# A fused attention and feed-forward kernel: strip one's first product taken set by set, three sets at two levels

## The chip, the cores and the metric

The kernel runs on one core of one Trainium2 chip. The metric is the device time of one execution in microseconds (us); the time of a kernel is the median of its runs. The engines are called as in the profile: PE (TensorE, the matmuls), PEld (its weight loads), DVE (VectorE), ACT (ScalarE), POOL (GpSimd) and SP (SyncE, which issues nearly all DMA transfers here).

## The reference

Everything is float32. An attention without softmax is followed by a feed-forward layer with a squared relu:

```python
# q, k, v: (8, 8, 576, 64); w_in: (512, 2048); w_out: (2048, 512)
kv = np.einsum('bhsd,bhse->bhde', k, v)
out = np.einsum('bhsd,bhde->bhse', q, kv)
rms = np.sqrt(np.mean(out * out, axis=-1, keepdims=True) + 1e-06)
out = out / rms * g_norm
x = out.transpose(0, 2, 1, 3).reshape(4608, 512)
h = np.maximum(x @ w_in, 0.0)
return (h * h) @ w_out
```

## The kernel before

**Strips.** The 4608 rows of x are 36 tiles of 128 rows, taken as nine strips of four tiles. Each strip has a first product (x with w_in, "up"), relu and square, and a second product (with w_out, "down"). While PE works on one strip, the attention that makes the next strips' x is slipped between its matmuls as *slices*: `transposed_query` (DVE turns a query tile), `key_value` (PE makes the 64 by 64 key-value products, ACT copies them), `query` (PE multiplies queries with them), then the mean, the inverse root and the scaling (DVE, or ACT for `scaled_heads`), and last either `features` (PE transposes the tile, ACT copies it into xT) or `squares_x` and `send_x` (DVE turns it in blocks of 32, the tile is stored to DRAM and later fetched back into xT by `fetch_x`). The list `slices` fixes their order; `attend(n)` issues them up to the n-th.

**Seven products for eight.** Every large product is computed by a Strassen-like scheme: x and w_in are cut in halves both ways, and seven products of sums and differences stand for eight. `A_IN` says in which of the seven blocks `b` of the tile `w_in` the operand of product `p` lies: 1:0, 2:2, 3:6, 4:3, 5:4, 6:5, 7:1. All blocks of all sets stay in the tile w_in. The quarters of the result are called 11, 12, 21 and 22 (tiles gt).

- *One level* (strip one before, `up`): for each of four column groups g, the seven products p in the order 1, 2, 6, 5, 7, 3, 4. Each has four matmuls with 128 by 128 weights and 256 columns of x. Three PSUM banks A, B, C collect them; ACT copies what is needed twice (snap), DVE adds two banks and applies relu and square in a second operation within SBUF.
- *Two levels* (strips two to eight, `up_slot` and `up_small`): the products are taken set by set, in the order `UP_SETS` = 1, 6, 7, 5, 2, 3, 4. Each set p is itself cut into seven small products j, of four matmuls with 128 columns. They are spread over 55 slots; set n takes the slots 7n, 7n+2, ..., 7n+12. A small product adds to what other sets left in the quarters (`UP_TO`), so no set has to be kept. The small products need sums of x (`sum_x`, `leaf_x`, on POOL) and, for j in 5, 6, 3, further sums of the weights.
- *Further sums of the weights* (`deep_sums_in(b)`, L1181): three POOL operations per block b make them from w_in, and one store (three for b = 0) writes them to the DRAM tensor w_in_deep, from which strips two to eight load them for each set. `deep_differences_in(b)` (L1200) overwrites one quarter of the block in w_in by a difference; it must come after every one-level use of the block and before its two-level use. Before the change the further sums are made during strip one (L1418, one block every third product, in the order b = 1, 6, 5, 4, 0, 2, 3) and the differences during strip two (L1253).

The second product of strips one to eight is `down_deep`: seven sets in the order 4, 1, 2, 6, 5, 7, 3, each of seven small products whose weights are read from DRAM (`w_blk`, two blocks per set of 0.79 and 1.05 MB, issued by `stream`). In strips two to eight the first three small products of its first set are issued within the last slots of up; in strip one before the change they are not.

**What sets the order.** There is no run-time scheduler: each engine works off its instructions in the order in which the loop at the end of the kernel (L1333 on) issues them, and waits on semaphores for operands and for buffers. SP issues the transfers in that order too, and each waits for the one eight places before it to land, so at most eight are under way. The pools matter: `stream_pool` has six buffers of 1 MB, shared by the w_blk blocks, the further sums while they are made, and the xT of each strip; `sum_pool` has eight buffers of 256 KB, for sums of x, of g (the operands of the second product) and parts of w_deep; `fpsum` has five PSUM banks from strip one on; the bank `x` that `query` writes is a single one. q, k and v loads are spread by a clock of the program's own (`clock`, `drip`, `keys_due`, `tiles_due`), which counts work issued, not time.

In strip one, before the change, the 28 steps of up and 14 of down are accompanied by this:

```python
if s == DEEP:
    attend(begun + (goal - begun) * min(i + 1, 25) // 25)
...
if s == 1 and i in range(2, 23, 3):
    deep_sums_in((1, 6, 5, 4, 0, 2, 3)[i // 3])
if s == 1 and i in (17, 20, 21, 23):
    stream()
```

Of the kernel before, what the change touches and what calls it, by code (L numbers as in the profile page):

```python
# [10 lines left out]
FP32 = mybir.dt.float32  # L11
# [9 lines left out]
def kernel(  # L21
# [34 lines left out]
    nc = tc.nc  # L56
# [593 lines left out]
    def send_x(n):  # L650
        d = sent[n] = dram.tile([P, 4, NP, SQ], FP32, name="x_d", tag="x_d", bufs=2 * NT)
        nc.sync.dma_start(out=d, in_=squared.pop(n))
        tiles_due.append((clock[0] + {9: 30, 10: 36, 11: 24}.get(n, 6), fetch_x, (n,)))

# [51 lines left out]
    slices += [(query_means, (last,)), (K, (2, 0, 1)), (T, (2, 0)), (roots_normalized, (last,)), (T, (2, 1))]  # L706
    slices += [(T, (2, 2)), (T, (2, 3)), (features, (last[0],)), (K, (2, 2, 3))]
    pair_ends = []
    for b in range(2, B):
        pairs = query_pairs(b)  # L710
        for i, pair in enumerate(pairs):
            left = len(pairs) - i
            more = b + 1 < B
            at = left + (b == 2)
            keys = (b + 1, *{2: (0, 1), 1: (2, 3)}[at]) if more and at < 3 else ()
            if i == 0 and b > 2:
                slices += [(T, (b, p)) for p in (2, 3)]
# [170 lines left out]

    def up(s, g, p):
        open_bank(p)  # L890
        rhs = {
            1: halves(s, 0, 0), 2: halves(s, 1, 0), 3: halves(s, 1, 1),
            4: xc[s][3], 5: xc[s][0], 6: xc[s][1], 7: xc[s][2],
        }[p]
        for i in range(2):
            product(p, i, lambda kc: w_in[:, kc, g, A_IN[p], ts(i, P)], lambda kc: rhs[:, :, kc, :], KH)
        dest = quarters(s, g)

        def relu_squared(q):
            def f(b, a):  # L900
                o = dest[q]
                nc.vector.tensor_tensor(out=o, in0=b, in1=a, op=ALU.add)
                nc.vector.scalar_tensor_tensor(out=o, in0=o, scalar=0.0, in1=o, op0=ALU.max, op1=ALU.mult)
            return f

        def last(b):
            nc.scalar.activation(dest[21], b, AF.Relu)
            nc.scalar.activation(dest[21], dest[21], AF.Square)

        combine(p, relu_squared(11), relu_squared(12), last, relu_squared(22))  # L910

# [190 lines left out]
    def down_deep(s, k, i):  # L1102
        p = DEEP_ORDER[k]
        if k == i == 0:
            stream()
        if s == N_STRIP - 1 and k == 6 and i == 1:
# [19 lines left out]
            return  # L1126
        if k == 0 and s >= DEEP_UP:
            if i == 0:
# [50 lines left out]
    w_half = lambda b, kc, f: w_in[:, kc, 2 * f : 2 * f + 2, b]  # L1179

    def deep_sums_in(b):  # L1181
# [7 lines left out]
        nc.gpsimd.tensor_tensor(out=s1, in0=w_half(b, 0, 1), in1=w_half(b, 1, 1), op=ALU.add)  # L1189
        minus(nc.gpsimd, s2, s1, w_half(b, 0, 0))  # L1190
        minus(nc.gpsimd, s4, w_half(b, 1, 0), s2)
        if b == 0:
            for n, x in enumerate((s1, s2, s4)):
                nc.sync.dma_start(out=w_in_deep[b, :, n], in_=x)
# [46 lines left out]
    def up_slot(s, slot):  # L1241

        for n, p in enumerate(UP_SETS):
            i, odd = divmod(slot - 7 * n, 2)
            if not odd and 0 <= i < 7:
                up_small(s, n, p, ORDER[i], slot)
# [86 lines left out]
    for s in range(N_STRIP):  # L1333
# [25 lines left out]
        for i, (w, fn, a) in enumerate(steps):  # L1359
# [33 lines left out]
            if s:  # L1393
                clock[0] += 3.2 if i >= n_up else 2.2 if s == DEEP else 1.2
                soon = tiles_due and tiles_due[0][2][0] // NT == s + 1
                if i == n_up + 10:
                    while tiles_due and tiles_due[0][2][0] // NT == s + 1:
                        _, f, a = tiles_due.popleft()
                        f(*a)
                elif not due(keys_due) and not (soon and due(tiles_due)):  # L1400
                    least = 2.1 if s == DEEP else 4.5 if i < n_up else 3.3
                    quiet = n_up * 2 // 3 < i < n_up + 3 or s == DEEP and i > n_up + 9
                    quiet = quiet or s == DEEP and i < n_up and drips and drips[0][0] == load_q_rest
# [15 lines left out]
                if s == 1 and i in (17, 20, 21, 23):  # L1419
                    stream()  # L1420
# [59 lines left out]
```

## Time and profile before

| what | value |
|---|---|
| median of 3 runs | 886.89 us (886.82 to 887.32) |
| profiled execution, its own time | 886.17 us |
| its span, first to last instruction | 884.4 us |
| granted clock of PE | 1.000 |
| strip one: up | 138.6 to 195.9 us |
| strip one: down | 195.9 to 236.9 us |
| strip two begins | 236.9 us |
| HBM read / written | 197.66 / 36.70 MB |
| mean transfer rate over the span | 265 GB/s |

The span runs from the first to the last instruction on the engines; the profiled execution's own time has 1.8 us more around it. Times in the views are counted from the start of the span. The chain of waits is followed back from the last instruction; where it runs through PE, PE had no time to spare. In it, and in counts of PE's instructions, every float32 matmul shows as two pieces.

### The profile page before, as it was taken

To read this page: it belongs to the slowest core of one execution; us is meant where nothing else is said; L and a number is where in the kernel's file an instruction comes from. 1 tells how busy PE (TensorE), PEld (TensorE's weight loads), DVE (VectorE), ACT (ScalarE), POOL (GpSimd) and SP (SyncE) were. 2 spreads that over 40 slices of the span, in tenths; PEclk is the share of its full clock that TensorE was granted. 3 is DMA by queue.
4 is the path that set the end of the run, shared out by engine and by line. 5 is a ranking of instruction groups with operands and counts; after the bars stand their busy time and mean duration, and the time that the engine had idled before them with its cause. 6 is when DMAs were issued, how large, how long until landed. Compare 5 with 4: busy or idle time off the path is not lost.

```text
span 884.4 us, 20899 instructions
## 1 busy us (share of the span) xinstructions
PE 876.4 (99%) x8296; PEld 822.1 (93%) x8296; DVE 721.9 (82%) x1239; ACT 351.8 (40%) x805; POOL 307.6 (35%) x316
## 2 busy tenths in 40 slices
PE   8999999999999999999999999999999999999998
PEld 7445888889999999999999999999999999999998
DVE  4999998879778985798778966897888778866887
ACT  4898242320048203740365034902491147102710
POOL 0000005610549133631474045604570447044700
PEclk9999999999999999999999999999999999999999
DMA  9998997999969996989677978897668765884482
GB/s 306 321 314 252 299 376 222 289 346 353 301 186 278 327 330 214 227 323 314 208 216 293 314 237 244 286 319 244 207 218 303 255 212 184 294 292 164 178 314 105
DMA packets 170257, 235.73 MB, mean 267 GB/s; under 512 B 79536, under 2 KB 134576, under 8 KB 161840
## 3 DMA queue, kind: packets, MB, share of 16 engines
q1 hardware_dynamic: 169856, 234.33, 81.0%
q8 instruction: 65, 1.06, 0.5%
q14 instruction: 32, 0.26, 0.1%
q10 hardware_dynamic: 304, 0.07, 0.0%
HBM read 197.66 MB, written 36.70 MB: 265 GB/s over the span
## 4 chain that ended last, share of the span: by engine, by line
PE 95%; DVE 2%; ACT 2%; issue 0%; POOL 0%; DVEq 0%; POOLq 0%
PE ps_B L1066 22%; PE ps_A L1283 19%; PE ps_A L1066 17%; PE ps_B L1283 9%; PE ps_A L839 6%; PE ps_C L1283 5%; PE ps_B L839 3%; PE kv_ps L432 2%; PE ps_A L880 2%; PE x_ps L468 2%; PE ps_C L839 2%; PE ps_C L880 2%; PE ps_B L880 1%; PE ps_A L617 1%; ACT gt L1234 0%
## 5 line engine op out<-in xcount | busy, mean ns | idle before, releaser
L1066 PE MATMUL ps_B<-w_blk,g_s 128*128 128x128 f32 x1008 | 123.9, 275 | 0.0
L1066 PEld LDWEIGHTS ps_B<-w_blk,g_s 128*128 128x128 f32 x1008 | 118.1, 192 | 0.1
L1283 PE MATMUL ps_A<-x_l,w_in 128*128 128x128 f32 x784 | 103.8, 275 | 0.3 <-ACT snap L1300 0.3
L289 POOL TENSOR_TENSOR x_l<-xT 128x256 f32<-128x256 f32 x21 | 15.7, 747 | 236.7 <-PE ps_A L1066 187.8
L1283 PEld LDWEIGHTS ps_A<-x_l,w_in 128*128 128x128 f32 x784 | 95.4, 192 | 0.6 <-ACT snap L1300 0.5
L1066 PE MATMUL ps_B<-w_blk,gt 128*128 128x128 f32 x752 | 95.2, 275 | 0.0
L1066 PE MATMUL ps_A<-w_blk,g_s 128*128 128x128 f32 x768 | 93.6, 275 | 0.0
L1066 PEld LDWEIGHTS ps_B<-w_blk,gt 128*128 128x128 f32 x752 | 89.6, 192 | 0.1
L1066 PEld LDWEIGHTS ps_A<-w_blk,g_s 128*128 128x128 f32 x768 | 89.6, 192 | 0.0
L1295 POOL TENSOR_TENSOR snap<-snap,gt 128x512 f32<-128x512 f32 x35 | 45.8, 1309 | 118.8 <-ACT snap L1300 103.7
L1300 ACT COPY snap<-ps_A 128x512 f32<-128x512 f32 x63 | 36.9, 585 | 109.7 <-PE ps_A L1283 98.0
L1233 ACT ACTIVATE gt<-gt 128x512 f32<-128x512 f32 x112 | 70.1, 625 | 12.8 <-DVE gt L1295 12.7
L1066 PE MATMUL ps_A<-w_blk,gt 128*128 128x128 f32 x576 | 72.2, 275 | 0.0
L1234 ACT ACTIVATE gt<-gt 128x512 f32<-128x512 f32 x112 | 70.7, 631 | 3.6
L1066 PEld LDWEIGHTS ps_A<-w_blk,gt 128*128 128x128 f32 x576 | 68.2, 192 | 0.0
L1082 ACT COPY o_sb<-ps_A 128x128 f32<-128x128 f32 x24 | 6.4, 265 | 148.4 <-PE ps_A L1066 148.4
L1081 DVE TENSOR_TENSOR o_sb<-o_sb,ps_B 128x256 f32<-128x256 f32 (+1 forms) x123 | 47.5, 386 | 16.9 <-ACT o_sb L1082 12.0
L289 DVE TENSOR_TENSOR gt<-gt 128x2048 f32<-128x2048 f32 (+1 forms) x29 | 59.7, 2064 | 0.0
L1295 POOL TENSOR_TENSOR gt<-gt,snap 128x512 f32<-128x512 f32 x42 | 52.3, 1273 | 17.8 <-DVE snap L1295 17.8
L1283 PE MATMUL ps_B<-x_l,w_blk 128*128 128x128 f32 x392 | 52.1, 276 | 0.0
L1283 PE MATMUL ps_A<-x_l,w_blk 128*128 128x128 f32 x392 | 51.9, 275 | 0.0
L1081 DVE TENSOR_TENSOR o_sb<-o_sb,ps_A 128x256 f32<-128x256 f32 (+1 forms) x96 | 37.2, 387 | 15.1 <-ACT o_sb L1082 10.5
(193 smaller groups left out, 1822.3 us busy)
## 6 DMA issues: line engine op xcount, KB each, us to landing
w_blk<-w_deep SPq DMA_DIRECT2D x56, 1024.0 KB, 6.6
w_blk<-w_out SPq DMA_DIRECT2D x56, 768.0 KB, 6.0
w_blk<-w_in_deep SPq DMA_DIRECT2D x49, 768.0 KB, 5.3
raw<-in_moe_w_in_dram SPq DMA_DIRECT2D x16, 512.0 KB, 7.1
raw<-in_moe_w_out_dram SPq DMA_DIRECT2D x16, 512.0 KB, 6.1
k<-in_k_dram SPq DMA_DIRECT2D x29, 256.0 KB, 4.6
v<-in_v_dram SPq DMA_DIRECT2D x29, 256.0 KB, 5.0
x_d<-x_q SPq DMA_DIRECT2D x27, 256.0 KB, 4.6
```

The source lines that it names most:

```text
L289: eng.tensor_tensor(out=out, in0=a, in1=b, op=ALU.subtract)
L432: nc.tensor.matmul(ps[ts(h, D), i], lhsT=a, rhs=w, start=i == 0 and c == 0, stop=c == C, skip_group_check=True)
L468: nc.tensor.matmul(ps[half, r, i, ts(p, D)], lhsT=q[row, half], rhs=kvd[b, p][row, row], start=True, stop=True)
L839: nc.tensor.matmul(bank[BANK[p]][:, i, :], lhsT=lhsT(k), rhs=rhs(k), start=p in (1, 5, 2) and i == 0 and k == 0, stop=k == n - 1, skip_gro ...
L880: nc.tensor.matmul(ps, lhsT=w_in[:, kc % KH, g, kc // KH * 2 + fh, ts(i, P)], rhs=xt[0][:, :, kc, :], start=kc == 0, stop=kc == NP - 1,)
L1066: nc.tensor.matmul(chain[c][x][:, i, :], lhsT=a[:, f, :], rhs=w[:, f, :], start=x not in opened[c] and f == 0, stop=f == FQ // 2 - 1, skip ...
L1081: add = lambda out, a, b: nc.vector.tensor_tensor(out=out, in0=a, in1=b, op=ALU.add)
L1233: nc.scalar.activation(o, o, AF.Relu)
L1234: nc.scalar.activation(o, o, AF.Square)
L1283: nc.tensor.matmul(ps[:, i, :], lhsT=w, rhs=rhs, start=j in (1, 2, 5) and i == 0, stop=True, skip_group_check=True)
L1295: add = lambda eng, out, a, b: eng.tensor_tensor(out=out, in0=a, in1=b, op=ALU.add)
L1300: nc.scalar.copy(t, ps)
```

## The change

Strip one's first product goes set by set. The sets 1, 6, 7 and 5 stay at one level: the new function `up_set(s, g, p)` runs the four matmuls of one group into one bank (ps_D), and adds from PSUM to the quarters (set 1 by an ACT copy; set 5 ends with relu and square of quarter 22 on ACT). The sets 2, 3 and 4 are done at two levels by `up_slot` in the slots 28 to 54, as in the later strips; the last three products of set 5 alternate with the first four slots. The first three small products of the second product's first set move into the slots 49, 51 and 53, so the weights for it are streamed earlier.

For this, the further sums of all blocks are made in another order and place (b = 6, 2, 3, 1, 5, 4, 0 at the steps 1, 3, 5, 7, 10, 13, 15), those of blocks 6, 2 and 3 stay in their stream buffers as weights of strip one, and the stores go out from a queue of their own some steps later. The differences of blocks 2, 6 and 3 move from strip two to strip one. A leaf of x is made for each of the three sets.

Around it, the attention of strip one changes: the first ten slices go one per product, the rest over the remaining 13 units of work; tile 8 goes through DRAM (`squares_x`, `send_x`, fetched when 50 units of the clock have passed) instead of `features`; the two pairs of batch two are scaled on ACT (`scaled_heads`) instead of DVE.

```diff
-        tiles_due.append((clock[0] + {9: 30, 10: 36, 11: 24}.get(n, 6), fetch_x, (n,)))
+        tiles_due.append((clock[0] + {8: 50, 9: 30, 10: 36, 11: 24}.get(n, 6), fetch_x, (n,)))
...
-    slices += [(T, (2, 2)), (T, (2, 3)), (features, (last[0],)), (K, (2, 2, 3))]
+    slices += [(T, (2, 2)), (squares_x, last), (T, (2, 3)), (K, (2, 2, 3)), (send_x, last)]
...
-                slices += [(T, (3, 1))] * (left == 1) + [(mean_roots, (pair,)), (normalized, (pair,))]
-                slices += [(T, (3, 0))] * (left == 2) + [(squares_x, (n,)) for n in pair]
+                slices += [(T, (3, 1))] * (left == 1) + [(mean_roots, (pair,)), (inverse, (pair,))]
+                slices += [(scaled_heads, (pair, t, r)) for t in range(2) for r in range(2)]
+                slices += [(T, (3, 0))] * (left == 2)
                 for n in pair:
-                    slices.append((send_x, (n,)))
+                    slices += [(squares_x, (n,)), (send_x, (n,))]
...
-    def up(s, g, p):
...
+    def up_set(s, g, p):
+        rhs = {1: lambda: halves(s, 0, 0), 5: lambda: xc[s][0], 6: lambda: xc[s][1], 7: lambda: xc[s][2]}[p]()
+        ps = fpsum.tile([P, 2, TH], FP32, name="ps_D", tag="f")
         for i in range(2):
+            for kc in range(KH):
+                nc.tensor.matmul(
+                    ps[:, i, :], lhsT=w_in[:, kc, g, A_IN[p], ts(i, P)], rhs=rhs[:, :, kc, :],
+                    start=i == kc == 0, stop=kc == KH - 1, skip_group_check=True,
+                )
         dest = quarters(s, g)
+        add = lambda q, a: nc.vector.tensor_tensor(out=dest[q], in0=ps, in1=dest[a], op=ALU.add)
+        if p == 1:
+            nc.scalar.copy(dest[11], ps)
+        elif p == 5:
+            add(22, 21)
+            add(12, 12)
+            nc.scalar.activation(dest[22], dest[22], AF.Relu)
+            nc.scalar.activation(dest[22], dest[22], AF.Square)
+        else:
+            add(*{6: (12, 11), 7: (21, 12)}[p])
...
-        if k == i == 0:
+        if k == i == 0 and s >= DEEP_UP:
             stream()
...
-        if k == 0 and s >= DEEP_UP:
+        if k == 0:
...
-            if k == 0:
-                nc.vector.tensor_tensor(out=q12, in0=q12, in1=q22, op=ALU.add)
...
+            if UP_SETS[4:].count(IN_SET[b]):
+                w_blk["in", DEEP, IN_SET[b]] = whole.rearrange("p n f e -> p n (f e)")
...
-        nc.sync.dma_start(
-            out=w_in_deep[b].rearrange("p n g e -> p n (g e)"), in_=whole[:, 0:3].rearrange("p n f e -> p n (f e)")
+        sums_to_store.append(
+            (w_in_deep[b].rearrange("p n g e -> p n (g e)"), whole[:, 0:3].rearrange("p n f e -> p n (f e)"))
         )
...
-        if s == DEEP_UP and at == 0 and n < 7:
+        if at == 0 and n < 7 and (s == DEEP_UP and n < 4 or s == DEEP and n > 4):
             deep_differences_in(A_IN[UP_SETS[n]])
...
-            steps = [(1, up, (s, g, p)) for g in range(NG) for p in ORDER]
+            x_sums[s, 4] = xc[s][3]
+            by_set = [(2, up_set, (s, g, p)) for p in UP_SETS[:4] for g in range(NG)]
+            small_ones = [(1, up_slot, (s, slot)) for slot in range(28, 55)]
+            steps = by_set[:13] + small_ones[:1] + by_set[13:14] + small_ones[1:3] + by_set[14:15]
+            steps += small_ones[3:5] + by_set[15:] + small_ones[5:]
...
-                    attend(begun + (goal - begun) * min(i + 1, 25) // 25)
+                    gone = min(int(passed[min(i, n_up - 1)]), 23)
+                    attend(begun + min(gone, 10) + max(gone - 10, 0) * (goal - begun - 10) // 13)
...
-                if s == DEEP and i == n_up - 3:
-                    leaf_sums(s, 4)
-                if s == 1 and i in range(2, 23, 3):
-                    deep_sums_in((1, 6, 5, 4, 0, 2, 3)[i // 3])
-                if s == 1 and i in (17, 20, 21, 23):
+                if s == DEEP and i in (1, 3, 5, 7, 10, 13, 15):
+                    deep_sums_in({1: 6, 3: 2, 5: 3, 7: 1, 10: 5, 13: 4, 15: 0}[i])
+                if s == DEEP and i in (3, 5, 7, 9, 11, 14, 26):
+                    for _ in range(3 if i == 26 else 1):
+                        out_ap, in_ap = sums_to_store.popleft()
+                        nc.sync.dma_start(out=out_ap, in_=in_ap)
+                if s == DEEP and i == 8:
+                    leaf_x(s, 4)
+                if s == DEEP and i == 9:
+                    deep_differences_in(2)
+                if s == DEEP and i in (18, 22):
                     stream()
```

More of the change, by code (lines that the diff above doesn't have):

```diff
@@ L887, in up_first @@
             nc.scalar.activation(dest[(11, 12, 21, 22)[2 * fh + th]][:, i, :], ps[:, ts(th, TH)], AF.Square)
-    def up(s, g, p):
[L890 to L894, printed above, removed]
-        for i in range(2):
-            product(p, i, lambda kc: w_in[:, kc, g, A_IN[p], ts(i, P)], lambda kc: rhs[:, :, kc, :], KH)
-        dest = quarters(s, g)
[L899 to L910, printed above, removed]
+    def up_set(s, g, p):
+        rhs = {1: lambda: halves(s, 0, 0), 5: lambda: xc[s][0], 6: lambda: xc[s][1], 7: lambda: xc[s][2]}[p]()
+        ps = fpsum.tile([P, 2, TH], FP32, name="ps_D", tag="f")
+        for i in range(2):
+            for kc in range(KH):
[3 more added lines that the diff above has]
+                )
+        dest = quarters(s, g)
+        add = lambda q, a: nc.vector.tensor_tensor(out=dest[q], in0=ps, in1=dest[a], op=ALU.add)
[8 more added lines that the diff above has]
+            add(*{6: (12, 11), 7: (21, 12)}[p])
     for p, t in zip((1, 2, 5), w_first):
@@ L1179 @@
     w_half = lambda b, kc, f: w_in[:, kc, 2 * f : 2 * f + 2, b]
+    IN_SET = {b: p for p, b in A_IN.items()}
+    sums_to_store = deque()
     def deep_sums_in(b):
@@ L1193, in deep_sums_in @@
             for n, x in enumerate((s1, s2, s4)):
-                nc.sync.dma_start(out=w_in_deep[b, :, n], in_=x)
+                sums_to_store.append((w_in_deep[b, :, n], x))
             return
-        nc.sync.dma_start(
-            out=w_in_deep[b].rearrange("p n g e -> p n (g e)"), in_=whole[:, 0:3].rearrange("p n f e -> p n (f e)")
+        sums_to_store.append(
+            (w_in_deep[b].rearrange("p n g e -> p n (g e)"), whole[:, 0:3].rearrange("p n f e -> p n (f e)"))
         )
@@ L1244, in up_slot @@
             i, odd = divmod(slot - 7 * n, 2)
-            if not odd and 0 <= i < 7:
+            if not odd and 0 <= i < 7 and (s > DEEP or n >= 4):
                 up_small(s, n, p, ORDER[i], slot)
@@ L1345 @@
         else:
-            steps = [(1, up, (s, g, p)) for g in range(NG) for p in ORDER]
+            x_sums[s, 4] = xc[s][3]
[3 more added lines that the diff above has]
+            steps += small_ones[3:5] + by_set[15:] + small_ones[5:]
+            small_steps = {28, 30, 32, 34, *range(35, 55)}
+            work = [2 if fn == up_set else a[1] in small_steps for _, fn, a in steps]
+            passed = [sum(work[: i + 1]) / 2 for i in range(len(steps))]
         n_up = len(steps)
@@ L1393 @@
             if s:
-                clock[0] += 3.2 if i >= n_up else 2.2 if s == DEEP else 1.2
+                clock[0] += 3.2 if i >= n_up else 1.1 * work[i] if s == DEEP else 1.2
                 soon = tiles_due and tiles_due[0][2][0] // NT == s + 1
@@ L1399 @@
                         f(*a)
-                elif not due(keys_due) and not (soon and due(tiles_due)):
+                elif not (due(keys_due) and (s > DEEP or due(keys_due) or True)) and not (soon and due(tiles_due)):
                     least = 2.1 if s == DEEP else 4.5 if i < n_up else 3.3
-                    quiet = n_up * 2 // 3 < i < n_up + 3 or s == DEEP and i > n_up + 9
+                    quiet = s > DEEP and n_up * 2 // 3 < i < n_up + 3
+                    quiet = quiet or s == DEEP and (i > n_up + 9 or i < n_up + 3 and passed[min(i, n_up - 1)] > 19)
                     quiet = quiet or s == DEEP and i < n_up and drips and drips[0][0] == load_q_rest
```

## The prediction

> **What bounds the kernel now.** I read the page's shares first: TensorE (PE) works 876.4 of 884.4 us, and the chain of waits is 95% PE. So a change pays where it takes work from PE, and costs where PE starts to wait. Then I took the stretch that is changed, strip one's first product, from the table of windows and the chain.
>
> ```profile
> PE 876.4 (99%) x8296; PEld 822.1 (93%) x8296; DVE 721.9 (82%) x1239; ACT 351.8 (40%) x805; POOL 307.6 (35%) x316
> ```
>
> ```profile
> 138.60:195.90 57.30, 57.27 (x511) 49.33 (x511) 45.90 (x71) 16.50 (x34) 29.62 (x21) 1.00 0.94 283
> 152.00:176.00 24.00, 23.96 (x204) 20.59 (x203) 20.27 (x32) 7.64 (x15) 15.78 (x12) 1.00 1.01 292
> 183.00:196.00 13.00, 13.00 (x63) 11.48 (x62) 10.39 (x20) 3.20 (x7) 0.00 (x0) 1.00 1.00 355
> ```
>
> The columns are the stretch, its length, then busy time (and count) of PE, PEld, DVE, ACT, POOL, the clock, the DMA share and GB/s. PE never stops in these 57.3 us, and neither do the DMA engines: share 0.94 to 1.01. PE and DMA are both full here; only ACT and POOL look free. The prices of PE's pieces come from the chain (start, duration, line, pieces; one float32 matmul counts as two pieces):
>
> ```profile
> 149.91 1.73 PE ps_B L839 x8
> 156.82 0.44 PE xt_ps L636 x4
> 158.98 1.46 PE kv_ps L432 x40
> 195.86 6.25 PE ps_B L1066 x56
> ```
>
> Four matmuls of 256 columns take 1.73 us. Seven products of four matmuls of 128 columns take 6.25, so one takes 0.893. What the other engines pay comes from their timelines, POOL's first, then a line each of ACT's and PE's:
>
> ```profile
> 142.77 1.27 POOL L1189 TENSOR_TENSOR w_i<-w_in 128x512 f32<-128x512 f32 x1 [58.81 <-DVE w_in L289]
> ...
> 147.04 1.71 POOL L1189 TENSOR_TENSOR w_i<-w_in 128x512 f32<-128x512 f32 x1
> ...
> 168.15 1.27 POOL L1189 TENSOR_TENSOR w_i<-w_in 128x512 f32<-128x512 f32 x1 [7.60 <-DMA w_deep<-w_t]
> ...
> 252.54 0.73 POOL L289 TENSOR_TENSOR x_l<-x_t 128x256 f32<-128x256 f32 x1
> 254.31 1.27 POOL L289 TENSOR_TENSOR w_in<-w_in 128x512 f32<-128x512 f32 x1
> ```
>
> ```profile
> 269.25 2.54 ACT L570 ACTIVATE x_n<-x_ps,newton 128x64 f32<-128x64 f32 x12
> ```
>
> ```profile
> 289.34 1.16 PE L1283 MATMUL ps_B<-x_t,w_blk 128*128 128x128 f32 x8 [0.40 <-DVE snap L1295]
> ```
>
> The line at 168.15 matters most: POOL already waits 7.6 us for a store to land before it may write the next sums. Today nobody needs those sums until strip two, so it is free. One set of three sums takes about 4.4 us (142.77, 147.04 and on); a leaf of x 1.77 (252.54 to 254.31); a difference of w_in 1.27.
>
> **The change, part by part.** *Sets 2, 3, 4 at two levels.* Before, a set is four groups of 1.73 = 6.90; after, 6.25. Three sets: -1.95 us on PE. *Tile 8* is transposed by DVE and sent through DRAM instead of through PE: -0.44 on PE; +0.67 DVE, one store and four fetches (0.5 MB), fetched about 209 to 226 as before and needed at about 238: nothing, and if that cover were gone it is the 4 to 6 us landing of an xT fetch. The three first pieces of strip one's second product only change places. So PE has 2.4 us less. No more can be gained but the 0.4 us of PE's wait in strip two (the last line above), where attention slices shift by a few slots: bounds -0.4 to +0.4, taken as nothing. One slice per product for the first ten brings the second key product from 159.0 to 156.7; its k and v loads lose a 0.79 MB store ahead of them (2.6 us at 308 GB/s) and stay ahead. Three differences leave strip two's POOL, which idles there: nothing.
>
> *DVE*: 24 operations of the sums and relu go (12 at L902 of 0.69; L903 averages 1.04), and 4 scalings; 34 of about 0.65 come. That is level, near 46 of 55 us. *ACT* gets 32 scaled heads (12 take 2.54, so 8 take 1.6) and 12 relu and square pairs (1.18 each at 268.05 and on) for what were 12 copies: about +17 us, nearly all of it in the last 25 us. *POOL* gets three leaves of x, three differences and, in the way of the sums, three snap adds and four adds of q22 to q12 (1.27 each): about +18 us. It starts no earlier, since the first set of sums needs DVE's last difference of w_in at 142.5.
>
> *SP's queue and the buffers.* Here the change adds a wait that decides. The stream pool has six buffers. Now xT and the sums of sets 2, 3 and 4 stay in four of them, as weights. By the instruction lists of the two kernels (built, not run), the seven sets of sums go through POOL in the order b = 6, 2, 3, 1, then leaf and difference, 5, leaf, 4, 0. The sums of b = 4 go into the buffer that b = 1 used, and wait for its store to land. That store stands in SP's queue behind 8 k and v loads (2.10 MB), 12 q loads (0.79), three stores of sums (2.36), one tile (0.26) and four stores of w_deep parts (1.05), together with itself 7.34 MB after the q load that lands near 152.0 (issued up to 150.1). At 292 to 316 GB/s (the windows 152 to 176 and 164 to 196) it lands at 177.1 to 175.2; I take 176.0. POOL without this wait would get there at 142.8 + 4x4.4 + 1.77 + 1.27 + 4.4 + 1.77 = 169.6. So it idles about 6 us.
>
> What PE does until then: thirteen products 22.4, query and key work 0.63 + 1.46 + 1.46 + 1.35, four re-entries of 0.2 (1.92 against 1.73): the first small product at 166.75. Four small and three large ones: 175.5. Key and query work 2.6, eight small ones 7.1: at 185.25 stands set 3's product 7, which reads the difference of w_in for set 3. POOL's order ahead of that: sums b = 4 (4.4), b = 0 (4.4), snap add 1.27, leaf 1.77, difference 1.27: 13.1 after 176.0 is 189.1. PE waits 3.8 us. DVE and ACT wait with it, so ACT's work no longer costs separately.
>
> *Behind it*: the store of b = 4 (issued when POOL is done, 180.4; 4.4 to land) blocks SP, and x_d, 0.79, x_d, 1.05, four k and v, 0.79 and the first store of b = 0 follow, 4.46 MB. At 355 to 370 GB/s (the last fence line of the windows, and 187 to 195.7) that store lands at 196.9 to 197.4. A further sum for DVE takes its buffer. DVE would be there at about 195.2; behind it on DVE stands the snap of set 4's product 5, 0.69 + 0.69 later, which PE needs for product 3 at 197.1. PE waits 1.1 to 1.7; I take 1.4, bounds 0 and 2.5.
>
> Sum: -2.4 + 3.8 + 1.4 = +2.8 us. The profiled execution took 886.17 (span 884.4 and 1.8 around it), 0.7 under the median 886.89 of the runs; on the median, **889.7 us**. A measurement of this kernel tells about 0.2%, 1.8 us, from no change.
>
> [...]
>
> [...]
>
> ```profile
> 142.46 0.68 DVE L902 TENSOR_TENSOR gt<-ps_C,snap 128x512 f32<-128x512 f32 x1
> 143.18 1.42 DVE L903 SCALAR_TENSOR_TENSOR gt<-gt 128x512 f32<-128x512 f32 x1
> 196.14 0.68 DVE L289 TENSOR_TENSOR g_s<-gt 128x512 f32<-128x512 f32 x1
> ```
>
> With POOL working, the add from PSUM takes 0.68 and the one within SBUF 1.42; with POOL idle the further sum takes 0.68. If all eight further sums before 200 doubled, DVE would lose up to 5.9 us, against 12 L903 that it no longer has; between 0 and 5.9, and hidden wherever PE waits for POOL anyway, I take nothing.
>
> **The rivals.** *POOL is in time, ACT sets the end* (not slower). If the store lands by about 172, PE first waits for ACT: from 170.5 its queue holds ten relu pairs 11.8, heads 6.4, three snap copies 1.5, key copies 0.5, squares 1.1, root 0.2 and about 1.3 idle for a mean, so the copy of set 4's product 6 ends at 193.3. PE wants to overwrite that bank at 191.5: +1.8. Sum -0.6, 886.3. It decides when the store lands before 185.25 + 1.8 - 13.1 = 174.0. For it: 355 GB/s in the later window; against: the 292 of the same stretch.
>
> *Nothing waits* (faster): the reserve of engines and queues holds, as it does in strips two to eight, where the same small products run with 0.4 us of waiting in all of strip two. -2.4: 884.5. Against: those strips make no sums and no stores of them.
>
> *The second product's weights come late* (slower): the blocked SP queue starves the w_blk blocks. Before, they land 3 to 4 us ahead of their use; if a block lands 2 us behind, once or twice, +2 to +4 on top of the forecast: about 893.
>
> *The change does not do what it says*: by the instruction lists the 48 matmuls of 256 columns are 84 of 128, so this one is out.
>
> **How the numbers follow.** The forecast's case (POOL behind the store of b = 1) gets 0.56: landing between 174 and 178 moves the first wait by -2 to +2, the second lies between 0 and 2.5, so -0.6 to +5.9; three quarters of that are over +1.8. ACT's case 0.25, of which nearly all is within 1.8. Nothing waits 0.11. Late weights 0.08. Slower 0.42 + 0.08 + 0.01 = 0.51, same 0.14 + 0.21 = 0.35, faster 0.03 + 0.11 = 0.14. For 8 in 10 the range goes from -1.2 (ACT's case and half of its own spread) to +6.0 (the forecast's case to its end): 885.7 to 892.9.
>
> **What would show it.** Right: in the changed profile POOL idles 4 to 8 us before a w_i operation, put down to a w_in_deep store; PE idles 2 to 5 us at a small product of strip one with w_in from POOL; DVE waits for a w_in_deep store before a further sum; the windows of strip one keep a DMA share near 1. Twelve groups of 1.73 that go and 21 of 0.89 that come confirm PE's gain. Wrong: POOL runs through without a gap (then I misjudged the queue), or PE's idle time in strip one is put down to ACT's copies (ACT's case) or to w_blk loads (late weights), or the end of strip one's first product stands 2 us or more earlier with no idle time on PE at all.

## The result and the profile after

| | us |
|---|---|
| changed kernel, median of 7 runs | 892.60 (891.19 to 896.63) |
| kernel before, median of 7 runs | 887.01 (885.63 to 888.95) |
| ratio, with its 95% interval | 1.0068 (1.0047 to 1.0089) |
| profiled execution of the changed kernel, its own time and span | 896.63 and 894.8 |

The change costs 5.6 us on the medians. The profiled execution is the longest of the seven, 10.4 us above the profiled one of before in span, so its rows show where the time goes, some of them larger than in a middling run. Where it went by strips, from the start of a strip's first matmul to the next strip's first, with the idle time of PE in it:

| | start of strip one | strip one (idle) | strip two (idle) | strip three (idle) | last strip, to the end |
|---|---|---|---|---|---|
| before | 138.63 | 98.16 (0.04) | 93.74 (0.40) | 92.26 (0) | 93.70 |
| after | 139.10 | 103.43 (5.56) | 97.57 (2.87) | 93.62 (1.13) | 93.18 |
| difference | +0.47 | +5.27 | +3.83 | +1.36 | -0.52 |

Strips four to seven are equal to 0.02 us, and the differences add up to 10.4. PE's row of the busy shares, against 876.4 before:

```profile
PE 877.0 (98%) x8364; PEld 824.6 (92%) x8364; DVE 720.6 (81%) x1245; ACT 369.3 (41%) x855; POOL 320.7 (36%) x332
```

PE was to work 2.4 us less and is busy 0.6 us more. The windows of the changed kernel say why (columns as before; the last but two is the granted clock):

```profile
139.20:204.30 65.10, 59.53 (x603) 53.82 (x602) 50.12 (x80) 32.10 (x82) 46.39 (x40) 0.97 0.91 293
204.30:242.70 38.40, 38.40 (x346) 38.40 (x346) 34.18 (x54) 3.91 (x10) 6.63 (x7) 1.00 0.84 300
242.70:340.00 97.30, 94.43 (x991) 93.61 (x991) 74.73 (x123) 36.93 (x89) 42.89 (x44) 0.98 0.88 265
...
178.90:182.00 3.10, 3.02 (x75) 2.93 (x76) 0.00 (x0) 1.40 (x5) 2.94 (x4) 0.53 0.80 217
182.00:184.00 2.00, 2.00 (x18) 2.00 (x17) 0.72 (x2) 0.46 (x1) 1.92 (x2) 0.88 0.64 267
...
260.60:264.00 3.40, 3.38 (x72) 3.26 (x73) 1.83 (x3) 1.09 (x2) 0.00 (x0) 0.56 1.10 335
```

The clock, 1.00 all through the kernel before, is 0.97 in strip one's first product. It is not low throughout: it falls to half in two places, from about 179 to 182.5 and for most of 260.6 to 264. What stands just ahead of them is in PE's timeline (in square brackets the idle time before a row, and what ended it):

```profile
178.98 0.33 PE L432 MATMUL kv_ps<-v_rest,k_rest 64*64 64x64 f32 x2 [2.00 <-DMA v_rest<-in_v_dram]
...
181.27 1.72 PE L1285 MATMUL ps_A<-xT,w_in 128*128 128x128 f32 x8
182.82 1.06 PE L1285 MATMUL ps_A<-x_l,w_in 128*128 128x128 f32 x8
...
190.11 1.16 PE L1285 MATMUL ps_A<-x_l,w_in 128*128 128x128 f32 x8 [0.87 <-POOL w_in L289]
...
197.70 1.13 PE L1285 MATMUL ps_A<-x_l,w_in 128*128 128x128 f32 x8 [1.07 <-ACT snap L1302]
...
201.34 1.16 PE L1285 MATMUL ps_B<-x_t,w_i 128*128 128x128 f32 x8 [1.62 <-DVE snap L1297]
...
260.62 0.34 PE L468 MATMUL x_ps<-kv_all,qT_rest 64*64 64x64 f32 x8 [2.87 <-DVE qT_rest L388]
```

Five waits, by four releasers. The two longest come first and last, and behind each the clock is at half: a small product starts 1.55 us before the next (181.27 to 182.82) where it otherwise takes 0.89. Of the five, the forecast had the second and the fourth. A sixth, of 1.13 us for a `w_blk` load, lies in strip three. POOL's timeline shows the wait that the forecast was built on, and DVE's the two that reach PE through it:

```profile
168.27 0.99 POOL L289 TENSOR_TENSOR x_l<-xT,x_l 128x128 f32<-128x128 f32 x2
177.95 1.26 POOL L1191 TENSOR_TENSOR w_i<-w_in 128x512 f32<-128x512 f32 x1 [8.69 <-DMA w_in_deep<-w_i]
...
188.79 1.27 POOL L289 TENSOR_TENSOR w_in<-w_in 128x512 f32<-128x512 f32 x1
```

```profile
192.96 1.80 DVE L289 TENSOR_TENSOR g_s<-g_s,gt 128x512 f32<-128x512 f32 x1
...
196.49 0.66 DVE L289 TENSOR_TENSOR g_s<-gt,g_s 128x512 f32<-128x512 f32 x1
...
199.28 1.40 DVE L289 TENSOR_TENSOR g_s<-gt 128x512 f32<-128x512 f32 x1 [1.53 <-DMA w_in_deep<-w_i]
...
259.26 0.71 DVE L384 STREAM_TRANSPOSE qT<-q 128x512 f32<-128x512 f32 x1 [6.00 <-DMA q<-in_q_dram]
```

POOL stands 8.69 us until the store of b = 1 has landed, and ends the difference for set 3 (188.79) when PE is waiting for it. DVE waits 1.53 for a store of b = 0. In strip two it waits 6 us for the last query tile of batch three: its second half is issued at 255.3, behind four fetches of xT and stores of out; before, both halves and q_rest were issued by 240.0 and DVE was done with qT_rest at 244.4. SP's queue shows what the two small loads stand behind, the store of b = 1 in strip one and the fetches in strip two:

```profile
171.73 0.52 SPq L1431 DMA_DIRECT2D w_in_deep<-w_i  x1
172.31 0.61 SPq L162 DMA_DIRECT2D k_rest<-in_k_dram  x1
172.97 1.34 SPq L162 DMA_DIRECT2D v_rest<-in_v_dram  x1
...
252.34 2.65 SPq L659 DMA_DIRECT2D xT<-x_d  x4
255.33 0.85 SPq L123 DMA_DIRECT2D q<-in_q_dram  x2
```

### The profile page after: what moved, and what is told of

Its sections match the earlier page's. It is cut to its first block, busy times and chain, and to the rows that moved or that the text cites. A ratio compares the mean times of both kernels' runs of the same rounds, so it can differ in the third digit from the quotient of the medians.

```text
span 894.8 us, 21126 instructions
## 1 busy us (share of the span) xinstructions
PE 877.0 (98%) x8364; PEld 824.6 (92%) x8364; DVE 720.6 (81%) x1245; ACT 369.3 (41%) x855; POOL 320.7 (36%) x332
## 3 DMA queue, kind: packets, MB, share of 16 engines
q8 instruction: 66, 1.08, 0.5%
## 4 chain that ended last, share of the span: by engine, by line
PE 79%; DVE 8%; DMA 6%; ACT 4%; issue 2%; SPq 1%; POOL 0%; DVEq 0%; ACTq 0%; POOLq 0%
PE ps_B L1065 22%; PE ps_A L1285 19%; PE ps_A L1065 17%; PE ps_B L1285 9%; PE ps_C L1285 5%; PE ps_D L895 2%; DMA w_in_deep<-w_i 2%; PE kv_ps L432 2%; PE x_ps L468 2%; DVE w_t L289 1%; ACT raw L254 1%; DMA w_deep<-w_t 1%; DMA q<-in_q_dram 1%; DVE wt L289 1%; ACT w_c L251 1%
## 5 line engine op out<-in xcount | busy, mean ns | idle before, releaser
L1285 PE MATMUL ps_A<-x_l,w_in 128*128 128x128 f32 x832 | 111.3, 277 | 2.3 <-ACT snap L1302 1.4
L1285 PEld LDWEIGHTS ps_A<-x_l,w_in 128*128 128x128 f32 x832 | 102.0, 193 | 3.0 <-issue 1.2
L1297 POOL TENSOR_TENSOR snap<-snap,gt 128x512 f32<-128x512 f32 x38 | 49.8, 1309 | 129.3 <-ACT snap L1302 119.5
L1235 ACT ACTIVATE gt<-gt 128x512 f32<-128x512 f32 x124 | 77.7, 626 | 14.6 <-DVE gt L1297 14.4
L1236 ACT ACTIVATE gt<-gt 128x512 f32<-128x512 f32 x124 | 78.2, 631 | 3.9
L1174 POOL TENSOR_TENSOR gt<-gt 128x512 f32<-128x512 f32 x32 | 52.8, 1668 | 0.0
```

Source lines behind the costliest of these rows:

```text
L1174: nc.gpsimd.tensor_tensor(out=a, in0=a, in1=b, op=ALU.add)
L1235: nc.scalar.activation(o, o, AF.Relu)
L1236: nc.scalar.activation(o, o, AF.Square)
L1285: nc.tensor.matmul(ps[:, i, :], lhsT=w, rhs=rhs, start=j in (1, 2, 5) and i == 0, stop=True, skip_group_check=True)
L1297: add = lambda eng, out, a, b: eng.tensor_tensor(out=out, in0=a, in1=b, op=ALU.add)
```

## The experiments

The theory after this reading: PE's saving is real, but small against four kinds of waits that hang on SP's queue (v_rest, POOL's buffer, DVE's buffer, qT_rest), and each of the two longest waits, 2.00 and 2.87 us, is followed by 3.41 us at half clock. The rival: the waits stand in for one another, since POOL, ACT and DVE are about as full as PE here (busy 8.4, 10.6 and 11.6 of the 12 us from 186 to 198, PE 10.1), so that taking one away brings out the next.

**The changed kernel again.**

> The changed kernel unaltered, run once more beside the others, so that they can be compared with it on one chip. If its waits are fixed by its order, the same five waits of PE in strip one (2.0 for v_rest, 0.9 for POOL, 1.1 for ACT, 1.6 for DVE behind a store) and the one of 2.9 in strip two for qT_rest come again, each within 0.5 us, and the time is again 5 to 6 us above the kernel before. If the profiled execution, at 896.63 the slowest of seven, was a chance, the waits of over 2 us shrink or go and the time is under 892.

895.1 us, ratio 1.0076 (1.0055 to 1.0096): 7.3 us above the kernel before on its chip, more than the 5 to 6 expected. The waits in strip one were 2.76 (v_rest), 2.27 (POOL) and 1.74 (DVE), in strip two 2.99 (qT_rest); none for ACT. So four of the five waits belong to the order, but they moved by up to 1.4 us from one execution to the next, more than the 0.5 expected.

**The small loads first.** `load_rest(3)` goes to strip one's first step.

```diff
-                if p == (1 if b > 3 else NP - 1) and b + 1 < B:
+                if p == (1 if b > 3 else NP - 1) and b > 2 and b + 1 < B:
...
+                if s == DEEP and i == 0:
+                    load_rest(3, nc.sync)
```

> Only k_rest and v_rest of batch three are loaded at the first step of strip one, ahead of the stores of the sums, instead of behind the store of b=1. Theory: the 2.0 us wait for v_rest goes, and with it the 3.2 us at half clock, so strip one is 3.8 us quicker up to there; but PE then comes to the difference of w_in for set 3 earlier than POOL, whose chain is tied to the landing of the store of b=1, so a wait for POOL of 3 to 4.5 us takes its place (the 3.8 of the forecast), and as it is over 2 us the clock falls there. Gain then 0 to 1 us. Rival: POOL's chain is itself held up by PE or by the two loads, and moves earlier with it; then the gain is 2 to 4 us and no new wait is over 1.5 us.

902.6 us, 7.5 above the changed kernel on the same chip. The wait for v_rest went, and POOL's took its place as expected, at 5.10 us where 3 to 4.5 were expected. But a second one of 7.26 us came, for DVE's snap behind the stores of b = 0, that no theory had:

```profile
190.27 2.07 PE L1285 MATMUL ps_A<-x_l,w_in 128*128 128x128 f32 x8 [5.10 <-POOL w_in L289]
...
207.25 2.08 PE L1285 MATMUL ps_B<-x_t,w_i 128*128 128x128 f32 x8 [7.26 <-DVE snap L1297]
```

SP's queue shows why:

```profile
184.00 0.98 SPq L652 DMA_DIRECT2D x_d<-x_q  x1
194.66 0.32 SPq L942 DMA_DIRECT2D w_blk<-w_deep  x1
```

The queue stands still for ten microseconds at a w_blk load; the profile puts 9.6 of them down to a small product on PE. In the instruction lists this load waits for the products of set 3 that read its further sums, in the changed kernel for those of set 2: with the two loads elsewhere the stream pool gave it another buffer. So this was not the clean removal of one wait. The four k and v loads and the stores of b = 0 stood behind it.

**b = 0 and b = 4 exchanged on POOL.** The sums of b = 0, which need no stream buffer, are made while POOL would stand.

```diff
-                    deep_sums_in({1: 6, 3: 2, 5: 3, 7: 1, 10: 5, 13: 4, 15: 0}[i])
+                    deep_sums_in({1: 6, 3: 2, 5: 3, 7: 1, 10: 5, 13: 0, 15: 4}[i])
...
-                    for _ in range(3 if i == 26 else 1):
+                    for _ in range(3 if i == 14 else 1):
```

> Only the further sums of b=0 and b=4 change places in POOL's order (and their stores with them): b=0, which needs no stream buffer, is made while POOL would wait for the store of b=1. Theory: POOL works 4.4 us in its idle time, the difference for set 3 is 4 us earlier, the stores of b=0 are issued early, so the waits of 0.87 (POOL) and 1.62 (DVE behind the store) go: about -2.5 us, and the 2.0 for v_rest stays or grows by up to 1 us, because the stores of b=0 are not ahead of it. Rival: the landing of the stores is set by the load of the DMA queues alone, so another wait of the same size opens behind it: 0 to -0.5 us.

892.07 us (1.0044, 1.0027 to 1.0061), 3.0 less than the changed kernel on that chip. Both waits were gone, as expected; 2.11 for v_rest stayed, and ACT's copy held PE 1.99 us instead of 1.07, which is the rival's part in it.

**Early query loads.** One `drip` per product more, in products 3 to 10 of strip one's second product.

```diff
+                if s == DEEP and n_up + 2 <= i <= n_up + 9:
+                    drip(True)
```

> Only the small query loads (q_rest and q of batch three) are issued one per product during products 3 to 10 of strip one's second product, in place of after the fetches of the tiles. Theory: the 2.87 us wait for qT_rest in strip two goes, and the half clock after it: -2.9 to -4.8 us, unless the loads of the second product's weights, which share SP's queue, come late by more than 0.5 us. Rival: the landing of those loads is not what DVE waited for, but its own queue; then the wait stays above 1.5 us and the gain is under 1 us.

893.03 us, 2.1 less than the changed kernel on that chip, where 2.9 to 4.8 were expected. No wait for qT_rest is left; strip two takes 93.08 us, 4.5 less than in the profile of after and 0.66 less than before. In this profile the wait for v_rest was 3.50, and a w_blk load came 0.62 late at the end of strip one.

**The exchange of POOL's sums and of the small loads.** To leave the numbering of the DMAs in place, k_rest and v_rest change places with two of the four stores of w_deep parts, so they stand ahead of the store of b = 1.

```diff
             for i, t in enumerate(parts):
+                if p == 4 and i > 1:
+                    later_parts.append((w_deep[B_OUT[p], :, i], t))
+                    continue
                 nc.sync.dma_start(out=w_deep[B_OUT[p], :, i], in_=t)
+            if p == 4:
+                load_rest(3, nc.sync)
...
-                    keys_later(load_rest, b + 1, nc.sync)
+                    keys_later(*(load_rest, b + 1, nc.sync) if b > 2 else (store_later,))
```

> The swap of b=0 and b=4, and also: k_rest and v_rest of batch three change places in SP's queue with two of the four stores of w_deep parts, so that they stand ahead of the store of b=1 and not behind it. Theory: the wait for v_rest (2.1 us with the swap alone) goes, and with it some 3.4 us at half clock, worth 1.7 us of work: 3.8 us less than the swap alone (892.07), 888.3, if PE is then not held elsewhere; the wait for ACT's copy of a snap, 2.0 us with the swap alone, may grow by as much as PE is early, so 888 to 891. Rival: the half clock costs nothing beyond the wait, because PE would be held behind it anyway: 890 to 892.

890.08 us (1.0017, 1.0002 to 1.0031), by the ratios 2.4 less than with the exchange on POOL alone (1.0044). In the profiles strip one goes from 101.91 to 98.72: the wait of 2.11 and the half clock behind it went, the 1.99 for ACT too, and 1.67 for POOL came. PE's timeline of this kernel:

```profile
187.41 1.16 PE L1296 MATMUL ps_A<-x_l,w_in 128*128 128x128 f32 x8 [1.67 <-POOL w_in L295]
...
255.79 0.49 PE L474 MATMUL x_ps<-kv_all,qT_rest 64*64 64x64 f32 x8 [2.65 <-DVE qT_rest L394]
```

**With the early query loads.**

> The same and the early issue of the small query loads of batch three in strip one's second product. Theory: the wait of 1.8 to 3.0 us for qT_rest in strip two goes too, with the half clock behind it where it is over 2 us; 2 to 4 us less than without: 885 to 888, at or below the kernel before (887.8 on that chip). Rival: the queue of weights is late by it and a wait for w_blk of 0.5 to 1 us takes its place, or ACT's wait holds PE in any case: 888 to 890, slower than the kernel before.

890.78 us (1.0027, 1.0014 to 1.0040). The rival held, and more than it said: the wait for qT_rest went, but w_blk came late in strip one, by 1.79 and 2.18 us. Eight loads more, ahead of the last weights, were too many.

**With the difference for set 3 made early.** `deep_differences_in(6)` at step 12, in POOL's idle time, in place of slot 35.

> The swap and the exchange of the small loads as before, and also: POOL makes the difference of w_in for set 3 at step 12, in its idle time, in place of behind the sums of b=0 and b=4. Theory: the last wait for POOL in strip one (1.67 us) goes, 1.2 to 1.7 us less than without (890.1): 888.4 to 888.9, if ACT's copy of the snap does not hold PE in its place. Rival: PE is early by that much at strip two's x_ps, and the wait there for qT_rest (2.65), whose loads are tied to SP's queue, grows by as much: no gain.

891.49 us (1.0034, 1.0022 to 1.0046): no gain, as the rival had it. POOL's wait went, and in strip two:

```profile
256.72 0.34 PE L474 MATMUL x_ps<-kv_all,qT_rest 64*64 64x64 f32 x8 [3.36 <-DVE qT_rest L394]
```

This wait, for qT_rest, grew from 2.65 to 3.36, and the clock behind it fell again: strip one is 0.5 shorter, strip two 0.9 longer.

**All waits moved away.** The last kernel and two more drips, behind the last weights of strip one:

```diff
+                if s == DEEP and i - n_up in (11, 13):
+                    drip(True)
```

> The same, and two of the small query loads of batch three are issued a step or two earlier, in the last products of strip one (n_up+11 and n_up+13), behind the last weights of that strip. Theory: the wait for qT_rest in strip two (2.65 us) and the half clock behind it (1.7) go, and no w_blk is late, as it was with eight early loads; with no wait of over 0.5 us left in strips one and two, what PE saves (2.4 us) shows at last: 884.5 to 886.5, quicker than the kernel before (888.1 on that chip). Rival: the eight DMAs more in the queue at the end of strip one make the first w_in_deep weights of strip two late: a wait of 1 to 2 us there, 887 to 889.

> The version with all waits moved away once more, so that its ratio to the kernel before has a narrower interval. Theory: PE saves 2.4 us and pays about 1.8 us of short waits in strip one for it, saves 0.4 in strip two and 0.5 in the last strip: 1 to 1.5 us quicker than the kernel before, as measured first (886.68 against 887.78). Rival: the first measurement was a lucky one; then 887.5 to 889, no quicker.

886.68 us at first (ratio 0.9990, 0.9973 to 1.0007), 887.39 the second time (0.9997, 0.9981 to 1.0013): level with the kernel before. The gain that both theories expected could not be measured. The windows of strip one's two products and of strip two:

```profile
139.40:204.00 64.60, 62.74 (x642) 56.89 (x641) 54.01 (x87) 34.56 (x87) 46.46 (x40) 1.00 0.93 297
204.00:237.90 33.90, 33.90 (x306) 33.90 (x306) 30.91 (x47) 1.33 (x5) 6.51 (x7) 1.00 0.93 329
237.90:331.30 93.40, 93.33 (x995) 92.47 (x994) 74.55 (x123) 36.96 (x89) 43.19 (x45) 1.00 0.91 285
```

The clock is 1.00 again and PE waits 1.86 us in strip one, 1.11 of it for ACT's copy of a snap. Without these waits strip one is 96.6 us, against 98.1 before: PE saves 1.5 us there and gives 1.9 back. The second profile has the same waits for ACT and DVE, and two for loads, 0.49 in strip one and 1.33 in strip two.

**The heads on DVE again.** Tiles 10 and 11 are scaled by two DVE operations, as before the change, instead of 16 on ACT.

```diff
+                if left == 1:
+                    slices += [(scaled, (pair, 0)), (nothing, ()), (scaled, (pair, 1)), (nothing, ())]
+                else:
```

> The version with all waits moved away, in which the second pair of batch two (tiles 10 and 11) is scaled on DVE again (two operations of about 0.7) and not on ACT (16 heads, 3.5 us): one part of the change undone. Theory: DVE has no gap from 183 to 198 either, so what ACT's copy of the snap no longer waits (1.1 us) comes back as a wait for DVE's snap behind the two scalings (now 0.4, then 1.0 to 1.8): within 0.5 us of the version without this edit. Rival: ACT alone held PE; then 1 us less, and no wait over 0.5 us in strip one.

887.92 us, against 887.39 of the version without this edit beside it (0.9998, 0.9984 to 1.0013, against 0.9997 to the kernel before). ACT's wait went and the two for DVE's snap grew, to 1.00 and 1.25 from 0.24 and 0.39. Taking the load from ACT brings out DVE, as the theory had it.

**The clock by itself.** Both holds are put into the kernel before. This is the long one; the short one has two additions and stands at k = 2 and 4:

```diff
+    def hold():
+        ps = apsum.tile([P, P], FP32, name="hold_ps", tag="at")
+        nc.tensor.matmul(ps, lhsT=ident, rhs=hold_t, start=True, stop=True)
+        for _ in range(6):
+            nc.gpsimd.tensor_tensor(out=hold_t, in0=hold_t, in1=hold_t, op=ALU.add)
+        nc.tensor.matmul(ps, lhsT=ident, rhs=hold_t, start=True, stop=True)
...
+        if 2 <= s <= 7 and i == 0 and k in (2,):
+            hold()
```

> The kernel before, in which PE is held once in the second product of each of strips two to seven (k=2): a 128-column matmul reads a tile, POOL adds it to itself six times (about 0.46 us each), and a second matmul reads it. The added work leaves the output alone. PE waits about 2.9 us each time, and the two matmuls take 0.45. Theory (a wait of 2 us or more is followed by some 3.4 us at half clock): each hold costs 2.9 + 0.4 + 1.7, six of them +30 us, and the windows behind each hold show a granted clock near 0.5. Rival (the half clock seen behind the waits was a chance of that place or of power): six times 3.3, +20 us, clock 1.0.

> The same, but with two holds in each of the strips two to seven (k=2 and k=4), each of two additions on POOL: PE waits about 1.1 us twelve times. Theory: no half clock behind such short waits; twelve times 1.1 + 0.4, +18 us, and a granted clock of 1.0. Rival (every wait costs clock in proportion to its length): +25 us and a clock under 1.0 behind each.

The long hold was 3.90 us, longer than planned, since the six additions on POOL came to 0.65 each. 929.5 us, so 41.4 for six, 6.9 each: 3.90 of waiting, 0.45 of matmuls, 2.5 more. The windows behind the first one:

```profile
308.80:312.20 3.40, 3.34 (x15) 3.34 (x16) 0.55 (x1) 0.00 (x0) 0.00 (x1) 0.50 0.47 115
312.20:314.00 1.80, 1.80 (x11) 1.80 (x10) 0.00 (x0) 0.00 (x0) 0.00 (x0) 0.50 0.00 0
314.00:318.00 4.00, 4.00 (x35) 4.00 (x35) 1.94 (x3) 0.27 (x1) 0.00 (x0) 0.93 0.51 180
```

Half clock for some 5 us behind the hold, which is the 2.5. The twelve short holds waited 1.01 to 1.08 us; 908.7, so 20.6 for twelve, 1.7 each: 1.05 and 0.45 and 0.2. The window behind the first short one:

```profile
305.20:308.00 2.80, 2.76 (x24) 2.76 (x25) 2.73 (x5) 0.00 (x0) 0.00 (x0) 1.00 0.89 275
```

Clock 1.00: the rival's proportional cost is out.

## Why the prediction was right and wrong

The forecast had the direction and the first link, and half the size: +2.8 us against +5.6, and against 10.4 in the profile. The step that failed by most is the term for strip two, "taken as nothing": it measured +3.83. In strip one the sum of 2.8 measured +5.27; there PE's saving was put too high, and two steps on other waits did not hold.

- *PE's saving, -2.4 in the sum: mis-sized.* In the version without half clock it is 1.5. The 224 pieces of seven one-level sets took 49.34 us before; 128 pieces of four sets and 168 of three took 28.43 and 19.41, so -1.50 and not -1.95: a piece of the small products takes 115.6 ns there and not 111.6 (6.25/56), and the large ones 222.1 and not 220.3. The 0.44 of tile 8's transposes went, but the second product's pieces, three products of which now stand between others, and the key products cost 0.65 more (41.52 against 41.09, 4.35 against 4.13), the queries 0.23 less. (Times from one matmul's start to the next, idle time left out.)
- *POOL behind the store of b = 1: right in cause, and within 2 us in time.* Forecast to idle about 6 us until 176.0; it idled 8.69 until 177.95. The transfers up to there ran at 302 GB/s (152.8 to 177.9), inside the 292 to 316 of the sum. *The 3.8 that this was to cost PE: right as a delay, not as a wait.* The product of set 3 for which PE waits starts 51.0 us after the start of the strip in the first profile and 52.0 in the second, but 46.4 to 47.1 in the versions that make the difference early. That is a delay of 3.9 to 5.7 us. Of it the wait for POOL is only 0.87 and 2.27, since PE had been held ahead of it by the wait for v_rest. With the small loads first, PE waits 5.10 for POOL and the product starts at 51.7, no earlier.
- *The loads of keys and values "stay ahead": failed.* The step looked at the second key product's k and v, which now come earlier, and not at k_rest and v_rest for the third, which stand in SP's queue right behind that very store of b = 1, by which the forecast had set its landing. PE waited 2.0 to 3.5 us for them. In the changed kernel this added little, because POOL would have held PE as long; it counts once POOL is in time, as with the exchange on POOL (2.11 and the half clock behind it).
- *No price for what a wait does to the clock: a missing term.* Strip one without its idle time is 97.87 us in the profile of after and 96.6 in the version without waits: 1.3 us, in strip two about as much. In strip one of the first profile this too lies ahead of POOL's end, inside the delay above (half clock from 179.1 to 182.5); in strip two nothing covers it.
- *"DVE and ACT wait with it, so ACT's work no longer costs separately": held only while PE's wait for POOL was long.* ACT held PE nowhere in the four profiles with a wait for POOL of 1.67 us or more. With a shorter wait or none it did: 1.07 us in the first profile, 1.99 with the exchange on POOL, 1.11 with all other waits gone. The rival's chain for ACT was sound: it had the copy end at 193.3, and in the last version it ends at 194.2.
- *The wait for the first store of b = 0, 1.4: right in cause, and near in size by luck.* It measured 1.62, though the store landed about 2 us later than said (199.3 against 196.9 to 197.4): DVE came as much later as well.
- *Strip two "taken as nothing", -0.4 to +0.4: failed*, and by most. +3.83 in the profile: 2.87 for qT_rest, less the 0.40 of before that is gone, and some 1.4 of half clock. It was read from PE's slack and the shift of slices, not from SP's queue: tile 8 goes through DRAM, and its fetch and those of the other tiles, later than before (214.1 to 228.1, where three stood at 202.5 to 218.6), each take the turn of one small query load. The last q_rest loads are issued at 243.4, before at 225.7. The step that said of tile 8's fetches "nothing" named their own landing and not who stands behind them. That the early drips alone bring strip two to 93.08, and the median down by 2.1, shows it.
- *DVE beside POOL, taken as nothing: the rows show a cost.* In the rows above a further sum takes 1.80 at 192.96, while POOL works (4.00 of the 4.00 us from 190 to 194), and 0.66 at 196.49, while POOL is idle (for 3.42 us until 197.63); before, with POOL idle from 181.1 to 229.9, 0.68 to 0.69 for all of them. In the version without the other waits the five from 187.5 to 196.6 take 6.3 us instead of 3.4. That it costs PE time is likely, since DVE has no slack there, but no run took it away by itself.
- *Late weights*, the slower rival: in the changed kernel only in strip three, by 1.13 us in the first profile and not in the second. In the other versions a load came up to 1.36 late there, 1.33 in strip two in the second profile of the version without waits, and 2.18 in the kernel with both exchanges and eight early loads.

## What to carry to other kernels

Where a change makes an idle engine and its stores part of the chain, list what else stands behind each moved transfer in its queue, and who waits for it up to one strip later: here the two longest waits were for small loads that the change did not touch. Read a wait as a delay at the product that is held, since an earlier wait can hide a later one: with the first wait gone, the next stood in its place. Price a wait of PE with what it does to the clock, and remove waits in full sets: the five versions that left one wait of over 2 us in strips one and two all stayed slower than the kernel before (ratios 1.0017 to 1.0058). And a saving on the fullest engine needs slack on the others: here PE's 1.5 us went to 1.9 us of short waits for ACT and DVE.

## What the hardware did that was not expected

Most waits of PE of 2 us or more cost more than their length, but not all: those of 2.00, 2.11, 2.18, 2.27, 2.65 and 2.87 us were followed by half clock, those of 2.76 and 2.99 in the second profile of the changed kernel were not. The records of the clock show a pattern. In the first profile of the changed kernel the granted clock changes at 179.06, 182.47, 260.98 and 264.39: two stretches of 3.41 us, whose starts lie 81.92 apart, 24 times 3.413. In the kernel with the long hold the half clock behind the six holds ends at 314.5, 413.6, 512.5, 614.9, 713.9 and 809.5, 28 to 30 times 3.413 apart. Cut into windows of that length, the profiles of before and after agree: in two windows PE stood idle 2.00 and 2.87 us, and the next one ran at half; in all others, some 510 between its first and last matmul, it stood idle 1.62 us or less, and the next one ran in full. So a wait that an edge of these windows cuts in two could pass. The second profile of the changed kernel has both cases (the 2.76 for v_rest lies in the first two rows, the 2.27 for POOL in the fourth):

```profile
175.93:179.34 3.41, 2.19 (x42) 1.91 (x40) 2.55 (x5) 3.35 (x8) 0.00 (x0) 1.00 1.07 354
179.34:182.75 3.41, 1.87 (x77) 1.83 (x78) 0.00 (x0) 1.88 (x5) 2.88 (x3) 1.00 1.05 295
182.75:186.17 3.42, 3.42 (x33) 3.42 (x32) 2.52 (x5) 0.64 (x2) 3.34 (x3) 1.00 0.59 219
...
189.58:192.99 3.41, 1.14 (x11) 1.12 (x11) 3.29 (x8) 3.35 (x11) 3.31 (x4) 1.00 1.00 408
192.99:196.41 3.42, 3.42 (x19) 3.42 (x18) 3.28 (x4) 3.39 (x15) 3.42 (x3) 0.50 1.05 383
```

The 2.76 is cut into 1.22 and 1.54 of idle time and costs no clock; the 2.27 lies within one window and is paid for with the next. The wait of 5.10 with the small loads first reached 0.4 us into the window at half, and the next one ran in full. The wait of 3.50 with the early query loads and five of the six of 3.90 reached 0.9 to 1.7 us into it, the next one ran at half too, and so there was half clock for over 5 us behind them.

Where the edges fall differs from one execution to the next: in the two profiles of the changed kernel one lies at 179.06 and one at 192.99, 4.08 times 3.413 apart. With them, the author's estimate is, the price of a wait differs. Of the twelve runs with both exchanges, five kept the clock at 1.00 (887.64 to 890.00 us) and seven had 0.998 (889.77 to 892.32), which is what one window of 3.41 us at half makes of 889. The medians of the two lie 3.3 us apart, of which a window at half explains 1.7; the rest stays open.
